# Weight pieces, routing places and scatters in the last attention half chunks: another order on four queues

## The chip, the cores and the metric

The kernel runs on one core of one Trainium2 chip. The metric is the device time of one execution in microseconds. Three timed runs of the kernel before are shown, and one more execution was taken with the hardware profiler.

## The reference

Three layers follow each other. What is computed, cut to the core:

```python
# 1. gated linear attention: B, H, S, D = 4, 8, 768, 48
f = 1 / (1 + exp(-f_logit))
for t in range(S):
    state = f[t][:, None] * state + outer(k[t], v[t])
    y[t] = q[t] @ state
x = y.reshape(3072, 384)
# 2. mixture of 8 experts, one per token, skipped where x @ w_skip <= 0
e = argmax(x @ w_gate);  gate_w = softmax(x @ w_gate)[e]
x = x + gate_w * (relu(x @ w1[e]) @ w2[e])
# 3. dense layer of width 2048
h = x @ w_in;  g = h * tanh(softplus(h));  out = g @ w_out
```

## The kernel before, in words

Every engine executes its own instructions in the order in which the program issues them; nothing is reordered. The order is written out by hand.

The attention runs in `attention` (L235 on) over 24 chunks `n` of 128 tokens; each chunk has two half chunks (two pairs of heads each), numbered `d` from 0 to 47. The loop at L676 covers `d` 0 to 43, and the last four are written out behind it (L776 to L812). For a half chunk TensorE does `stage1(d + 2)` (scores, L373, which ScalarE copies out and GpSimd masks, L386) and `stage2(d)` (L418 with the running state `sbd`, then L426 and L438). ScalarE's `evac(d)` (L470) copies the outputs out, VectorE's `state(d)` (L459 to L465) makes the state that `stage2(d + 2)` reads. In program order `state(d - 1)` stands at the head of half chunk `d`. Each even `d` VectorE also makes `kg` and `kh` (L344 to L352), GpSimd makes a query tile (`qh`, L357), and TensorE turns the chunk before into rows (`finalize`, L482 to L490).

Routing goes by groups of chunks (L675): `(first chunk, chunks, half chunk of route1, lag)`. The groups (0, 7), (7, 7) and (14, 4) are ranked at `d` = 17, 31 and 39. There TensorE counts ranks (`rank`), VectorE computes `place` (three small operations, L562 to L564: an expert's limit for each token, and the position of a token without an expert) and `rank_read` (four, L571 to L574, the last one a copy of the position into the token's row). One half chunk later `route2_all` (L590 to L598) gives the slots, and GpSimd's indirect DMAs (`scatter`, issued at L233) write the rows into the DRAM tensor `tokens`, one for each chunk, one per half chunk for a group of seven and two per half chunk for the group of four (`d` = 40 and 41). Chunks 18 to 20 are ranked behind the loop, at `d` = 44, and chunks 21 to 23 later still.

`first_x` (called at `d` = 42) loads the first 128 rows of two experts from `tokens` on SyncE's queue (`load_half`, L853). `transposed` (L840) turns them: three transposes on TensorE, a copy on ScalarE (L848), a residual on VectorE (L849). The attention's call of it stands at `d` = 46. The first expert matmuls (`half1`, L922) read its result.

`Weights` (L70 on) brings weights in chunks of three pieces of 512 columns. `step` makes one piece: ScalarE copies it to a rounded upper part (L131), VectorE subtracts that from the raw piece (L116, 128x512, the residual). A residual is kept pending until the next `step`, so that ScalarE's copy has time; at a chunk's last piece it is not kept, so two residuals stand together there. Steps with `load=False` run at `d` = 34 to 43 (`W_AT`), one at 44, one at 46 and two at 47. `load` issues the next chunks on SyncE's queue as soon as their stage buffer has been read.

Of the kernel before, what the change touches and what calls it, by code (L numbers as in the profile page):

```python
# [15 lines left out]
ALU = mybir.AluOpType  # L16
# [8 lines left out]
NT = B * NC  # L25
# [7 lines left out]
GATE, POS, TOK = DM, DM + 1, DM + 2  # L33
# [31 lines left out]
class Weights:  # L65
# [22 lines left out]
    def load(self):  # L88
        now = self.pieces[self.piece][1] if self.left() else len(self.chunks)
        while self.loaded < min(len(self.chunks), now + len(self.stage)):  # L90
            src, o, width, wide = self.chunks[self.loaded]
            t = self.stage[self.loaded % len(self.stage)]
            s = src[:, o:o + width]
            if wide:
                self.nc.sync.dma_start(out=t.bitcast(U32), in_=s.bitcast(U32))
            else:
                self.nc.sync.dma_start(out=t, in_=s)
            self.loaded += 1
# [19 lines left out]
    def step(self, eng=None, load=True, now=False):  # L118
        nc = self.nc
        eng = eng or nc.vector  # L120
        if not self.left():
            self.flush(eng)
            return
        u, c, o, so, n, last = self.pieces[self.piece]
        wide = self.chunks[c][3]
        st = self.stage[c % len(self.stage)]
        hi_t, lo_t = self.dests[u]
        hi, lo = hi_t[:, o:o + n], lo_t[:, o:o + n]
        if not wide:
            raw = st[:, so:so + n]  # L130
            nc.scalar.copy(hi, raw)  # L131
        self.flush(eng)
        if wide:
            v = st.bitcast(U32)[:, 2 * so:2 * (so + n)].rearrange("p (n t) -> p n t", t=2)
            low, high = v[:, :, 0], v[:, :, 1]
            t = self.tmp["t"]()
            nc.vector.tensor_scalar(t, high, 3, 0x3FFFFFF8, ALU.logical_shift_left, ALU.bitwise_and)
            nc.vector.scalar_tensor_tensor(t, high, 0xC0000000, t, ALU.bitwise_and, ALU.bitwise_or)
            nc.vector.scalar_tensor_tensor(t, low, 29, t, ALU.logical_shift_right, ALU.bitwise_or)
            raw = t.bitcast(F32)  # L140
            if now:
                nc.scalar.copy(hi, raw)
                eng.tensor_tensor(lo, raw, hi.bitcast(F32), ALU.subtract)
        if not (wide and now):
            self.pend = (lo, raw, hi)
            self.late = wide
        self.piece += 1
        if last:
            if not wide:
                self.flush(eng)  # L150
            if load:
                self.load()
# [88 lines left out]
def attention(tc, A, st, weights, open_weights, open_second, first_x):  # L241
    nc = tc.nc
    kqT, fT, v, U = A["kqT"], A["fT"], A["v"], A["U"]
    const = st["const"]
# [8 lines left out]
    pr = tail.enter_context(tc.tile_pool(name="at_pr", bufs=1, space=PSUM, side="right"))  # L253
# [213 lines left out]
    def evac(d):  # L467
        n, h2 = divmod(d, 2)
        ot, _ = ous[d]
        nc.scalar.copy(xts[n % 2][K112, 2 * h2:2 * h2 + 2, :], ot[K112])  # L470
        if h2 == 1:
            del prep[n]
# [83 lines left out]
        row = rows[n // RG][:, n % RG:n % RG + m, :]  # L556
        nc.gpsimd.tensor_copy(row[:, :, TOK:UW].bitcast(U32), tok.to_broadcast([128, m, UW - TOK]))

    def place(n, m):
        oh, pos, oh_lim = rt[n][0], rt[n][3], rt[n][4]  # L560
        p = pos[:, :, 0]
        nc.vector.tensor_tensor(oh_lim, oh, const["lim"][:, 0:m, :], ALU.mult)  # L562
        nc.vector.tensor_tensor(p, oh[:, :, 7], const["rtok"][:, n:n + m], ALU.mult)
        nc.vector.tensor_tensor(p, p, const["place"][:, n:n + m], ALU.add)  # L564

    def rank_read(n, m):
        oh, t, ex, pos, oh_lim = rt[n]
        rk = rks[n]
        t2 = rks[n] = small("t2", m, 8)
        row = rows[n // RG][:, n % RG:n % RG + m, :].bitcast(U32)  # L570
        nc.vector.tensor_tensor(pos[:, :, 0], pos[:, :, 0], rk[:, :, 7], ALU.subtract)  # L571
        nc.vector.tensor_tensor(t, rk, oh_lim, ALU.is_lt)
        nc.vector.tensor_tensor(t2, rk, bc(pos), ALU.subtract)
        nc.vector.tensor_copy(row[:, :, POS], pos[:, :, 0])  # L574

    def route2(n, m):
        oh, t, ex, pos, oh_lim = rt[n]
# [25 lines left out]
    def scatter(n):  # L603
        scatter_rows(tc, "tiles", st, U, st["slot"][:, n:n + 1], rows[n // RG][:, n % RG, :])

    def pad():
        p = pr.tile([1, EARLY], F32, name="pad", tag="fin", bufs=1)
        cum = st["cum"]
        nc.tensor.matmul(p, lhsT=const["ones"][:, 0:1], rhs=cum[:, 0:EARLY], start=True, stop=True)
        nc.vector.tensor_scalar(p, p, -1.0, float(CAP // 2), ALU.mult, ALU.add)  # L610
        c = cum[0:1, 0:EARLY]
        nc.vector.scalar_tensor_tensor(c, p, 0.0, c, ALU.max, ALU.add)
# [63 lines left out]
    for d in range(ND - 4):  # L676
        n, h2 = divmod(d, 2)
        if d - 4 in SIGMOID_AT:
            table(LN_EXP)
        ranked = [r for r in group if d == r[2] + r[3]]  # L680
        fresh = h2 == 0 and 0 < n < NT - 2 and d - 2 not in SIGMOID_AT
        if fresh:
            recip(n + 2)
        while h2 == 0 and asked < min(NT, n + (3 if d < QUERY_AT else 4)) and ready(asked, d):
            qh(asked)
            asked += 1
        if d > 0:
            state(d - 1)
        if fresh:
            kg(n + 2)  # L690
            kh(n + 2)
        if d - 1 in SIGMOID_AT:
            kg(n + 3)
            kh(n + 3)
        if d > 0:
            if d == 2:
                keep_warm(14)
            stage1(d + 2, all(d - i not in SIGMOID_AT for i in (1, 2)))
        for r in group:
            if d == r[2] + 1:  # L700
                route_exp(*r[0:2])
        if h2 == 0 and n >= 1:
            finalize(n - 1)
        stage2(d)
        if d == 0:
            keep_warm(3)
            stage1(2, True)
        for r in ranked:
            rank(*r[0:2], d=d)
        evac(d)  # L710
        for r in ranked:
            place(*r[0:2])
            rank_read(*r[0:2])
        for d0, pair in SIGMOID_AT.items():
            if d0 < d < d0 + 4:
                for i, p in ((0, 0), (0, 2)) if d == d0 + 1 else ((1, 2 * (d - d0 - 2)),):
                    sigmoid(pair[i], p, p + 2)
            for hh, at in zip(pair, SCAN_AT[d0]):
                if d - d0 in at:
                    p = 2 * at.index(d - d0)  # L720
                    scan(hh, p, d % 2)
                    scan(hh, p + 1, d % 2)
                if d - d0 == at[1]:
                    ends(hh)
        if d in SIGMOID_AT:
            recip(n + 3)
            if asked == n + 3:
                qh(asked)
                asked += 1
            table(SIGMOID)  # L730
        if d == 0:
            ends(0)
            qh(2)
            asked = 3
        if d == 1:
            scan(1, 2, 0)
            scan(1, 3, 0)
            kg(2)
            kh(2)
            ends(1)  # L740
            const.update(route_consts(tc, st["cp"], wk))
        if d % 6 == 1 and d // 6 + 2 < NH:
            load(d // 6 + 2)
        if d in F_AT:
            load_f(4 + F_AT.index(d))
        if d in ZERO_AT:
            zero(ZERO_AT.index(d))
        if d == LOAD_AT:
            weights.load()
        if d == CLOSE_AT:  # L750
            early.close()
            open_weights()
        if d == SECOND_AT:
            mid.close()
            open_second()
        if d in W_AT:
            weights.step(load=False)
        if d in LOADS_AT:
            weights.load()
        for r in group:  # L760
            if d == r[2]:
                route1(*r[0:2])
            elif d == r[2] + r[3] + 1:
                route2_all(*r[0:2])
            elif d == r[2] + 1:
                tokens(*r[0:2])
        if d == ND - 5:
            pad()
        if d == ND - 6:
            x = first_x()  # L770
        for r in group:
            for i in range(r[1]):
                if d == r[2] + r[3] + 1 + (i // 2 if r[1] == 4 else i):
                    scatter(r[0] + i)
    st["x0T"] = [wk.tile([128, KD, 128], F32R, name=f"x0T{i}") for i in range(2)]
    d = ND - 4  # L776
    route1(NT - 6, 3)
# [21 lines left out]
    d += 1  # L799
    stage2(d)  # L800
    evac(d)
    transposed(tc, st, pr, x[0][:, 0, :], *st["x0T"], slice(0, 128), "ut")
    finalize(NT - 2)
    weights.step(load=False)
    d += 1
    stage2(d)
    evac(d)
    for i in range(2):
        weights.step(load=False)
# [6 lines left out]
    finalize(NT - 1)  # L816
    route1(NT - 3, 3)
    route_exp(NT - 3, 3)
    place(NT - 3, 3)
    tokens(NT - 3, 3)  # L820
    yield
    rank(NT - 3, 3)
# [805 lines left out]
```

## Time and profile before

| | us |
|---|---|
| median of 3 runs | 724.15 |
| lowest and highest run | 721.01, 724.60 |
| the profiled execution | 722.45 |
| its span, first to last instruction | 720.1 |
| TensorE matmul busy | 686.9 (95%) |
| VectorE, ScalarE, GpSimd busy | 529.5, 500.1, 166.5 |

The page gives times of the profiled execution; the 2.35 us between its span and its time lie outside the instructions. The attention with its tail takes the first 154 us. Times in views are microseconds from the span's start. PE is TensorE, DVE VectorE, ACT ScalarE, POOL GpSimd, SP SyncE. An entry in square brackets is the idle time of the engine before the instruction, with what ended it.

### The profile page before, as it was taken

Reading aid. Unit: us, or ns where it says so; the run is one execution under the profiler, and the core shown is the slowest. Engines: PE = TensorE matmul, PEld = TensorE weight load, DVE = VectorE, ACT = ScalarE, POOL = GpSimd, SP = SyncE. Lnnn points to the kernel's source line nnn. Section 1 sums busy time; section 2 is a strip of 40 time slices with the busy share of each in tenths; the row PEclk is TensorE's granted clock in tenths of the full one; section 3 lists DMA queues with packets and bytes.
Section 4 is the critical chain, followed back from the end, with each engine's and each line's share of the span. In section 5 each row is a group of like instructions: output and inputs, shape, how many; then the busy total and the mean of one; then the engine's idle time right before and its main releaser. Section 6 shows DMA issues by size and latency. Waiting matters only on the chain.

```text
span 720.1 us, 13033 instructions
## 1 busy us (share of the span) xinstructions
PE 686.9 (95%) x5000; PEld 618.7 (86%) x5000; DVE 529.5 (74%) x1049; ACT 500.1 (69%) x857; POOL 166.5 (23%) x219
## 2 busy tenths in 40 slices
PE   6988889799999999999999999999999999999994
PEld 3777777687999999989998999999999999989994
DVE  6678889977668889879988875766556656666571
ACT  5689778566656654398989867767776686658671
POOL 4643857634001111212222220200020001002002
PEclk8999999899999999999999999999999999999998
DMA  9577834358468874602241112212232133100001
GB/s 351 231 285 268 337 127 174 133 166 294 148 232 263 272 281 154 231 25 88 88 132 45 44 45 89 88 49 84 89 132 87 45 94 127 45 1 34 11 1 48
DMA packets 24790, 97.88 MB, mean 136 GB/s; under 512 B 3476, under 2 KB 10080, under 8 KB 23696
## 3 DMA queue, kind: packets, MB, share of 16 engines
q1 hardware_dynamic: 20272, 83.88, 34.0%
q0 software_dynamic: 4448, 13.09, 4.9%
q8 instruction: 41, 0.67, 0.4%
q14 instruction: 29, 0.24, 0.1%
HBM read 81.88 MB, written 15.84 MB: 136 GB/s over the span
## 4 chain that ended last, share of the span: by engine, by line
PE 73%; issue 1%; DVE 1%; DMA 1%; POOLq 0%; POOL 0%; ACT 0%
PE y L1144 28%; PE h L1094 27%; PE y L908 8%; PE h L893 7%; PE pt L847 2%; PE h L922 1%; DMA x<-tokens 1%; PE h L934 0%; POOLq L1624 0%; DVE hs L1107 0%; DVE wB L849 0%; POOL tokens L233 0%; DVE wB L848 0%; POOLq L1571 0%; DVE gl L1127 0%
## 5 line engine op out<-in xcount | busy, mean ns | idle before, releaser
L1108 ACT ACTIVATE sp<-hs 128x512 f32<-128x512 f32 x96 | 59.7, 628 | 73.6 <-DVE hs L1107 72.8
L1094 PE MATMUL h<-wB,wB 128*128 128x512 f32 x432 | 108.9, 396 | 0.0
L1094 PE MATMUL h<-wB,wA 128*128 128x512 f32 x432 | 106.8, 393 | 0.0
L1144 PE MATMUL y<-wD,gh 128*128 128x384 f32 x384 | 98.9, 339 | 0.0
L1144 PE MATMUL y<-wA,gh 128*128 128x384 f32 x384 | 97.6, 335 | 0.0
L1125 DVE TENSOR_TENSOR hs<-hs,sp 128x512 f32<-128x512 f32 x96 | 69.8, 727 | 32.5 <-ACT sp L1119 32.4
L1094 PEld LDWEIGHTS h<-wB,wA 128*128 128x128 f32 x432 | 80.3, 188 | 14.3
L1094 PEld LDWEIGHTS h<-wB,wB 128*128 128x128 f32 x432 | 79.5, 188 | 14.5
L1107 DVE COPY hs<-h 128x512 f32<-128x512 f32 x71 | 48.9, 688 | 41.0 <-PE h L1094 40.8
L1127 DVE TENSOR_TENSOR gl<-hs,gh 128x512 fp32r<-128x512 f32 x96 | 67.3, 701 | 13.5 <-PE y L1144 6.4
L1144 PEld LDWEIGHTS y<-wA,gh 128*128 128x128 f32 x384 | 70.0, 188 | 4.2
L1144 PEld LDWEIGHTS y<-wD,gh 128*128 128x128 f32 x384 | 70.5, 188 | 3.4
L1144 PE MATMUL y<-wD,gl 128*128 128x384 f32 x192 | 65.1, 339 | 0.0
L1144 PE MATMUL y<-wA,gl 128*128 128x384 f32 x192 | 64.5, 336 | 0.0
L1115 ACT ACTIVATE sp<-sp,tiny 128x512 f32<-128x512 f32 x96 | 61.8, 713 | 0.3
L373 PE MATMUL at<-qi,kh 48*128 48x176 f32 (+1 forms) x384 | 43.5, 348 | 10.1 <-DVE lg L490 6.5
L1119 ACT ACTIVATE sp<-sp 128x512 f32<-128x512 f32 x96 | 52.9, 621 | 0.3
L233 POOL DMA_INDIRECT out<-stage,idx x24 | 23.8, 993 | 124.7 <-ACT stage L1163 62.1
L1126 DVE CAST gh<-hs 128x512 fp32r<-128x512 f32 x96 | 48.8, 509 | 3.3
L877 ACT ACTIVATE mhh<-h 128x256 fp32r<-128x256 f32 x64 | 23.7, 383 | 32.9 <-PE h L893 25.8
L373 PEld LDWEIGHTS at<-qi,kh 48*128 48x128 f32 x384 | 31.2, 201 | 15.8 <-POOL qi L357 3.4
L1173 POOL COPY idx<-rows 128x2 uint32<-128x2 uint32 x12 | 3.3, 290 | 156.5 <-DMA rows<-tokens 156.5
(216 smaller groups left out, 1443.7 us busy)
## 6 DMA issues: line engine op xcount, KB each, us to landing
stage<-in_w SPq DMA_DIRECT2D x64, 768.0 KB, 4.5
kq<-in_kqT SPq DMA_DIRECT2D x6, 1536.0 KB, 6.8
rows<-tokens SPq DMA_DIRECT2D x16, 388.0 KB, 5.1
fb<-in_fT SPq DMA_DIRECT2D x8, 768.0 KB, 9.4
vb<-in_v SPq DMA_DIRECT2D x7, 576.0 KB, 9.5
tokens<-zeros SPq DMA_DIRECT2D x4, 776.0 KB, 9.3
kq<-in_kqT SPq DMA_DIRECT2D x2, 1024.0 KB, 9.2
kq<-in_kqT SPq DMA_DIRECT2D x2, 512.0 KB, 7.8
```

Of the source, the lines that this page charges most:

```text
L373: nc.tensor.matmul(at[:, j, a * QW:a * QW + w], lhsT=k[r, p, :], rhs=q[r, p, 0:w], start=True, stop=True)
L893: nc.tensor.matmul(h, lhsT=w[:, o:o + 128], rhs=x[:, k, :], start=(k == 0 and i == 0), stop=(k == KD - 1 and i == 2),)
L908: nc.tensor.matmul(ys[e, a], lhsT=h, rhs=w[:, ws], start=(f == 0 and i == 0), stop=(f == NE - 1 and i == 2),)
L1094: nc.tensor.matmul(h, lhsT=w[:, o:o + 128], rhs=x[:, k, :], start=(k == 0 and i == 0), stop=(k == KD - 1 and i == 2),)
L1107: (nc.scalar.copy if busy(s) else nc.vector.tensor_copy)(hs, h)
L1108: nc.scalar.activation(out=sp, in_=hs, func=AF.Sigmoid, scale=-1.0)
L1115: nc.scalar.activation(out=sp, in_=sp, func=AF.Ln, bias=st["tiny"])
L1119: nc.scalar.activation(out=sp, in_=sp, func=AF.Tanh, scale=-1.0)
L1125: nc.vector.tensor_tensor(hs, hs, sp, ALU.mult)
L1126: nc.vector.tensor_copy(gh, hs)
L1127: nc.vector.tensor_tensor(gl, hs, gh.bitcast(F32), ALU.subtract)
L1144: nc.tensor.matmul(ys[b][a], lhsT=g[:, a * 128:(a + 1) * 128], rhs=w, start=(first and i == 0), stop=(fs[-1] + 1 in ends and i == len(ins) ...
```

## The change

Five edits, all in the order or the engine of small work:

- `rank_read` writes the position into the row by a subtraction of its own, first of the four operations, where a copy stood last.
- `place` runs on GpSimd for the groups ranked at `d` = 17, 31, 39 and 44; the last group keeps VectorE.
- A chunk's last residual is kept pending like the others in steps with `load=False`; `load` flushes it if its stage buffer is about to be overwritten.
- The four scatters of the group (14, 4) go one at `d` = 40, two at 41, one at 42, and `first_x` at 42 stands behind them.
- The first rows are turned at `d` = 47 between `stage2` and `evac`, where they were turned at 46 behind `evac`.

```diff
     def load(self):
         while self.loaded < min(len(self.chunks), now + len(self.stage)):
+            if self.pend is not None and self.pieces[self.piece - 1][1] == self.loaded - len(self.stage):
+                self.flush(self.nc.vector)
...
         if last:
-            if not wide:
+            if not wide and (load or eng is not nc.vector):
                 self.flush(eng)
...
-    def place(n, m):
+    def place(n, m, eng=nc.gpsimd):
-        nc.vector.tensor_tensor(oh_lim, oh, const["lim"][:, 0:m, :], ALU.mult)
-        nc.vector.tensor_tensor(p, oh[:, :, 7], const["rtok"][:, n:n + m], ALU.mult)
-        nc.vector.tensor_tensor(p, p, const["place"][:, n:n + m], ALU.add)
+        eng.tensor_tensor(oh_lim, oh, const["lim"][:, 0:m, :], ALU.mult)
+        eng.tensor_tensor(p, oh[:, :, 7], const["rtok"][:, n:n + m], ALU.mult)
+        eng.tensor_tensor(p, p, const["place"][:, n:n + m], ALU.add)
...
     def rank_read(n, m):
+        nc.vector.tensor_tensor(row[:, :, POS], pos[:, :, 0], rk[:, :, 7], ALU.subtract)
         nc.vector.tensor_tensor(pos[:, :, 0], pos[:, :, 0], rk[:, :, 7], ALU.subtract)
         nc.vector.tensor_tensor(t, rk, oh_lim, ALU.is_lt)
         nc.vector.tensor_tensor(t2, rk, bc(pos), ALU.subtract)
-        nc.vector.tensor_copy(row[:, :, POS], pos[:, :, 0])
...
+        for r in group:
+            for i in range(r[1]):
+                if d == r[2] + r[3] + 1 + ((i + 1) // 2 if r[1] == 4 else i):
+                    scatter(r[0] + i)
         if d == ND - 6:
             x = first_x()
-        for r in group:
-            for i in range(r[1]):
-                if d == r[2] + r[3] + 1 + (i // 2 if r[1] == 4 else i):
-                    scatter(r[0] + i)
...
     evac(d)
-    transposed(tc, st, pr, x[0][:, 0, :], *st["x0T"], slice(0, 128), "ut")
     finalize(NT - 2)
     weights.step(load=False)
     d += 1
     stage2(d)
+    transposed(tc, st, pr, x[0][:, 0, :], *st["x0T"], slice(0, 128), "ut")
     evac(d)
...
-    place(NT - 3, 3)
+    place(NT - 3, 3, nc.vector)
```

## Rows read from the trace of the kernel before

**Rows 1.** Busy time of each engine by stretch; instructions in brackets, granted clock behind
```profile
core 0: us, PE busy (x) PEld busy (x) DVE busy (x) ACT busy (x) POOL busy (x), PEclk, DMA share, GB/s
117.30:132.40 15.10, 13.91 (x226) 11.46 (x221) 13.85 (x31) 13.59 (x28) 14.17 (x15) 1.00 0.35 121
132.40:135.60 3.20, 0.00 (x0) 0.00 (x0) 3.20 (x4) 0.79 (x2) 2.36 (x3) 1.00 0.15 56
135.60:143.40 7.80, 7.18 (x76) 6.55 (x78) 7.45 (x23) 3.78 (x8) 3.63 (x4) 0.56 0.46 154
143.40:153.60 10.20, 10.20 (x177) 8.82 (x173) 8.17 (x36) 6.68 (x16) 5.02 (x7) 1.00 0.47 157
```

**Rows 2.** Waits of PE, 118 to 154 us: total, times, longest
```profile
PE ou L418 <- DVE sbd L465: 3.3, 1, 3.3
```

**Rows 3.** Timeline of DVE, 128 to 136 us: start, duration, what, count
```profile
128.47 1.48 DVE L116 TENSOR_TENSOR wB<-stage,wB 128x512 fp32r<-128x512 f32 x1
129.88 0.34 DVE L465 TENSOR_TENSOR sbd<-ou,sbd 112x192 f32<-112x192 f32 x1
130.14 0.35 DVE L562 TENSOR_TENSOR ohl<-oh,lim 128x32 f32<-128x32 bf16 x1
...
131.71 3.60 DVE L116 TENSOR_TENSOR wB<-stage,wB 128x512 fp32r<-128x512 f32 x2
135.23 0.34 DVE L465 TENSOR_TENSOR sbd<-ou,sbd 112x192 f32<-112x192 f32 x1
```

**Rows 4.** Line 116's instructions: duration in ns, least, median, most
```profile
L116 DVE TENSOR_TENSOR wB<-stage,wB x36: 678/683/2564, 117.1 to 251.2; 128x512 fp32r<-128x512 f32 x36
```

**Rows 5.** Timeline of POOL, 128 to 136 us
```profile
128.09 1.28 POOL L357 TENSOR_TENSOR qi<-kq,fb 112x512 f32<-112x512 f32 x1
129.31 1.13 POOL L386 TENSOR_SCALAR_AFFINE_SELECT am<-am 128x512 f32<-128x512 f32 x1
...
131.83 0.66 POOL L386 TENSOR_SCALAR_AFFINE_SELECT am<-am 128x512 f32<-128x512 f32 x1
132.44 1.27 POOL L357 TENSOR_TENSOR qi<-kq,fb 112x512 f32<-112x512 f32 x1
133.66 1.10 POOL L386 TENSOR_SCALAR_AFFINE_SELECT am<-am 128x512 f32<-128x512 f32 x1
```

**Rows 6.** Groups of POOL to 160 us by shape: busy us, mean ns, idle before
```profile
L357 POOL TENSOR_TENSOR qi<-kq,fb 112x512 f32<-112x512 f32 x24 | 31.2, 1301 | 4.3 <-DVE fb L297 3.6 <-DMA kq<-in_kqT 0.5
...
L318 POOL TENSOR_SCALAR f<-eend 112x4 f32<-112x4 f32 x8 | 1.8, 223 | 0.7
...
L557 POOL CAST xr<-tok 128x8 uint32<-128x8 f32 x1 | 0.2, 213 | 0.0
```

**Rows 7.** Timeline of POOL and DVE around the ranking at half chunk 17
```profile
68.52 0.65 POOL L386 TENSOR_SCALAR_AFFINE_SELECT am<-am 128x512 f32<-128x512 f32 x1 [0.65 <-ACT am L383]
...
69.09 0.21 DVE L562 TENSOR_TENSOR ohl<-oh,lim 128x56 f32<-128x56 bf16 x1
...
69.69 0.16 DVE L571 TENSOR_TENSOR pos<-pos,ou 128x7 f32<-128x7 f32 x1
```

**Rows 8.** Timeline of DVE at the ranking of half chunk 31
```profile
108.81 0.16 DVE L571 TENSOR_TENSOR pos<-pos,ou 128x7 f32<-128x7 f32 x1 [0.17 <-ACT xts L470]
```

**Rows 9.** Timeline of ACT and PE where the first expert matmuls start
```profile
151.49 0.48 ACT L848 CAST x0T<-pt 128x384 fp32r<-128x384 f32 x1
...
153.59 0.38 ACT L470 COPY xts<-ou 112x256 f32<-112x256 f32 x1
...
154.02 0.74 PE L922 MATMUL h<-wB,x0T 128*128 128x512 f32 x2 [0.34 <-ACT xts L470]
```

**Rows 10.** Timeline of POOL and SP: last scatter of group (14, 4), first row loads
```profile
143.47 0.98 POOL L233 DMA_INDIRECT tokens<-xr,slot  x1 [0.30 <-issue]
...
146.54 0.80 SPq L853 DMA_DIRECT2D x<-tokens  x2
```

**Rows 11.** DMA issues of the page: count, KB each, median us to landing
```profile
x<-tokens SPq DMA_DIRECT2D x2, 194.0 KB, 2.5
```

## The prediction

> **What bounds the kernel now.** I read the busy time by stretch first. From 117.3 to 132.4 us POOL is busy 14.17 of 15.10 us, PE 13.91, DVE 13.85 and ACT 13.59: four full queues that feed each other. From 132.4 to 135.6 PE does nothing at all. From 135.6 to 143.4 PE is busy 7.18 of 7.8 us, but for 76 matmuls only, and its granted clock is 0.56, so mostly the lower level of 1.2 GHz, right behind that idle time; DVE is busy 7.45 us there. From 143.4 PE is busy without a gap at the full clock [rows 1]. So the place where a reordering can gain is the gap and what follows it. Secondly the waits of PE: in 118 to 154 us its one long wait is 3.3 us, in the second state matmuls (L418) for `sbd` of L465 [rows 2].
>
> The timeline of DVE then shows what stood ahead of that L465: the `state` of half chunk 38 ends at 130.22, `place` and `rank_read` of 39 run from 130.14 to 131.71, and then two residuals take 3.60 us instead of two times 0.68, the first of them 2.56 [rows 3, 4]. The timeline of POOL says why: the masking L386 and the query product L357 run back to back from 131.83 to 133.71, and DVE's first residual ends 0.56 us behind them, at 134.27; the second ends behind the next L386, which itself took 1.10 instead of 0.66 [rows 3, 5]. The residual of 128.47 tells the same: it ends at 129.95, 0.58 behind POOL's L357 (129.37), and POOL's next L386 is stretched to 1.13 [rows 3, 5]. So an operation of DVE on two SBUF tiles and POOL's work exclude each other, and the loser waits for whole instructions.
>
> **Part by part.** *Place on POOL, half chunk 39.* DVE loses three small operations, 0.6 us by those of half chunk 17 (69.09 to 69.69, [rows 7]). POOL gets three, of a kind without a row of its own. From below: 3 x 0.21, the small cast and scalar operations there [rows 6], 0.63 us. From above: these plus the slope of L357, (1.30 - 0.21) / 512 = 2.1 ns for each of up to 56 elements, 0.33 a piece, 1.0 us. I take 0.8, nearer to the small rows, since two of the three have 7 elements or fewer. POOL is in order, so they stand behind the masking of the same half chunk, which ends at 132.49 [rows 5]: places are ready at 133.3. `rank_read` on DVE waits for them, and queued behind it are the residual and the `state` of half chunk 39, for which PE waits. DVE, which worked from 130.22 on, now idles until 133.3. Then `rank_read` (four of at most 0.16 [rows 7], taken as 0.5) to 133.8, and one residual instead of two. By then POOL runs the query product, moved by the 0.8 from 132.44 to 133.3, to 134.55; the residual ends 0.56 behind it, at 135.1. The state, 135.23 before, starts at 135.05: **-0.2 us**. What the second residual would have cost (1.04 of the 3.60) is given up to the wait for places. Ends: if the residual loses to the next mask too, as it did to two in a row at 131.71, that adds 0.65, so +0.5. If POOL comes to 39 earlier by a stretched instruction or two (0.45 each, 1.10 or 1.13 against 0.66), state starts 0.9 earlier, and the gap may be short enough for the clock to stay: -0.9 minus the price of the clock.
>
> That price: the matmuls of 135.6 to 143.4 took 7.18 us at 0.56 and would take 4.0 at full clock, but DVE was busy 7.45 of the 7.8 us, so between 0.35 and 3.2 us [rows 1]; I take 1.5, near the middle, because no row favours an end.
>
> The Trainium skill ("SBUF — State Buffer", section "Who interferes with whom") says that whoever issues first gets the shared port pair for its whole instruction, and the other blocks. The residual issued at 131.71, ahead of the mask at 131.83, lost to it and to L357 behind it [rows 3, 5], so the trace doesn't bear the rule out there; by the rule the residual would end at 135.1, by the row at 135.75. The skill's "GPSIMD Engine Reference" (section "Engine selection") speaks against the edit: elementwise work with two inputs is about 2x slower on GpSimd. By that, an estimate from the 0.6 us of DVE, places take 1.2 us, and the sum would be 0.8 higher (0.4 at 17 and at 39); no row shows such an operation on POOL.
>
> *Place on POOL, half chunks 17, 31, 44.* At 17 POOL's mask ends at 69.17, so places are ready at 69.97, and `rank_read` starts at 70.05 instead of 69.69 [rows 7]: **+0.36**, ends 0.2 and 0.55 by the two prices; all on DVE's path, and I find no idle time of DVE soon behind it that would take it up; below nothing is excluded, as DVE would only wait. At 31 POOL is free long before; but DVE's L571 waits for ACT's L470 there in any case, 0.17 us [rows 8], so the time freed turns into a longer wait: 0, at best the -0.6 of the operations if that wait belongs to another cause. At 44 PE is busy throughout [rows 1]: 0; if DVE's relief shows or POOL's place is late, within 0.3 either way.
>
> *No two residuals together.* The count of residuals is unchanged; those of pieces 2, 5 and 8 move one step later. At 36 one moves away and at 37 one is added before `route1`, where POOL is just as full; it delays DVE by about one residual, 0.7 us, up to half chunk 38, where the residual waits for POOL's L357 in any case [rows 3, 5]: 0. If that cover is gone, 0.7 us. At 40 residual 5 now stands before `route2_all`, so slots and the next states come 0.7 us later; PE, slow there, hides it, and at full clock some 0.4 would show. SP's loads of the next chunks wait one step longer; their pieces are used several steps later: 0.
>
> *Positions without a copy.* Four operations before, four after, each 0.16: 0. The first instead of the last writes the row and reads PSUM, so it can't collide with POOL: between -0.3 and 0.
>
> *Scatters one, two, one.* Each takes POOL 0.98 us [rows 10]. One moves from 40 to 41 and one from 41 to 42. Masks for the following half chunks come earlier by one scatter at 41 and are otherwise unmoved. The last scatter starts some 1.2 us later, by the 0.7 of the slots and about 0.5 of POOL's order: 144.7 instead of 143.47. SP's `first_x` started 3.07 us behind the last scatter (146.54) [rows 10] and lands 2.5 us after issue [rows 11]: 147.8 and 150.3. What is queued behind it on SP are chunk loads, not urgent.
>
> *First rows turned later.* PE does the same transposes one `finalize` and one `stage2` later, about 1.7 us, at 152.6: 2.3 us behind the landing. ACT's copy (0.48) now stands before `evac` of 47 instead of well ahead of it; PE's first expert matmul waited for that `evac` (153.59 + 0.38, then 154.02) [rows 9]. In the old order ACT was itself held up by DVE's residual of the first rows, which now comes later, so I expect the row copy from about 0.5 us earlier, the new copy to 153.65 and `evac` to 154.0: **+0.1**, ends 0 and +0.5 (the whole copy on the path).
>
> **Sum:** -0.2 + 0.36 + 0 + 0.1 = +0.25 us. The profiled execution's 722.45 would be 722.7; the median of the runs lies 1.7 above that execution, so 724.15 becomes **724.4**.
>
> **Rivals.** *The gap closes.* If POOL's places came before DVE needs them at 39 (POOL ahead by about 2.5 us, or places issued while POOL waits for something), one residual without a collision would put the state at about 132.5. The gap of 3.3 us and the price of the clock, 1.5, go: -4.8, so 719.35. For it: two residuals of 3.60 us are the direct cause of the gap. Against it: POOL has no free time from 117.3 on [rows 1], and the mask ahead of the places ends at 132.49 [rows 5].
>
> *Half of it.* POOL comes 0.9 us earlier and the clock stays up: -0.9 - 1.5 and the rest of the sum, +0.45: 722.2, still within 0.5%.
>
> *Slower: the first rows come too late.* The last scatter, `first_x` behind it and the transposes are now one chain, and `evac` of 47 stands behind the transposes' copy on ACT. If the landing comes after 152.6, PE waits, and nothing else is queued on it. It decides from 2.3 us of delay on: one more POOL collision for each of the three scatters and two masks ahead (5 x 0.45) and a scatter slower to land by 2.3 would make it 2.3 us late, and a second fall of the clock costs up to another 1.5: 724.4 + 3.8 = 728.2. Against it: the margin, and POOL's idle time in this stretch (5.02 of 10.20 busy, [rows 1]).
>
> **How the numbers follow.** Forecast 0.55 (with the ends of its costs, 722.7 to 726), the gap closes 0.2, half of it 0.12, too late 0.13. A measurement of this kernel tells about 0.5%, 3.6 us, from no change. The gap closing is the one case beyond it on the fast side, the late rows on the slow side: faster 0.2, same 0.67, slower 0.13. The range takes in the gap closing with the -0.6 of half chunk 31, 718.8, and most of the way to the late rows, 727.2.
>
> **What would show it.** Right: PE still waits over 2 us for L465 near 133 to 135.5, DVE's idle time before the first `rank_read` operation is ended by POOL, the residual behind it still takes over 1 us, and the clock falls behind it. At 17, DVE waits about 0.4 us for POOL. Wrong: places on POOL of 0.1 us or of 0.5 us each; a residual of 0.68 at 39 and no gap; PE waiting for x at the late transposes; or a fall of the clock at another place.

## The result and the profile after

| | before | after |
|---|---|---|
| median of six runs each, us | 724.07 | 731.18 |
| lowest and highest, us | 720.97 to 724.60 | 726.94 to 733.63 |
| ratio, 95% interval | | 1.0104 [1.0066, 1.0143] |
| the profiled execution, us | 722.45 | 728.95 |
| its span, us | 720.1 | 727.3 |

The changed kernel is slower by 7.1 us, outside the range of the prediction (718.8 to 727.2). Lines of the changed file stand 2 below those of before (L116 is L118, L465 is L467, L847 is L849).

First the stretch that the prediction was about. Busy time by stretch in the kernel after (columns as in [rows 1]), then the timelines of DVE and of POOL at half chunk 39, which answer to [rows 3] and [rows 5]:

```profile
132.40:135.60 3.20, 2.77 (x42) 2.45 (x38) 2.08 (x7) 1.80 (x5) 3.12 (x6) 0.83 0.17 62
135.60:143.40 7.80, 6.28 (x105) 5.44 (x105) 7.59 (x24) 5.17 (x11) 3.94 (x5) 1.00 0.46 152
```

```profile
133.49 0.16 DVE L573 TENSOR_TENSOR xr<-pos,ou 128x4 uint32<-128x4 f32 x1 [2.31 <-POOL pos L566]
...
133.98 1.24 DVE L118 TENSOR_TENSOR wB<-stage,wB 128x512 fp32r<-128x512 f32 x1
135.15 0.34 DVE L467 TENSOR_TENSOR sbd<-ou,sbd 112x192 f32<-112x192 f32 x1
```

```profile
132.16 0.65 POOL L388 TENSOR_SCALAR_AFFINE_SELECT am<-am 128x512 f32<-128x512 f32 x1
132.78 0.24 POOL L564 TENSOR_TENSOR ohl<-oh,lim 128x32 f32<-128x32 bf16 x1
132.98 0.19 POOL L565 TENSOR_TENSOR pos<-oh,rtok 128x4 f32<-128x4 bf16 x1
133.25 0.20 POOL L566 TENSOR_TENSOR pos<-pos,place 128x4 f32<-128x4 f32 x1
133.40 1.27 POOL L359 TENSOR_TENSOR qi<-kq,fb 112x512 f32<-112x512 f32 x1
```

DVE idles 2.31 us for the places, the one residual behind them still loses to POOL's query product (1.24 us, and its end at 135.22 is 0.55 behind POOL's 134.67), and the state starts at 135.15, where it was 135.23. That is DVE's wait as it was predicted. PE's is another one in this profile: it waits only 0.43 us for that state, because it comes there late itself, with its clock at the lower level from 130.05 to 133.46 us. Nothing is lost up to here: the first expert matmul starts at 154.11 against 154.02 in [rows 9].

The loss lies behind. The waits of PE from 160 to 310 us, before and after (total, times, longest):

```profile
PE pt L847 <- DMA x<-tokens: 1.4, 2, 1.0
```

```profile
PE pt L849 <- DMA x<-tokens: 4.1, 1, 4.1
PE pt L849 <- DMA rows<-tokens: 1.6, 1, 1.6
...
```

Two places, then. *Place 1* is near 174 us: PE waits for `x`, the second halves of the rows of the first two experts, which GpSimd loads behind the last scatters (chunks 21 to 23). The chain that leads there, in the kernel after (start, duration):

```profile
167.92 4.84 issue
172.76 4.90 DMA x<-tokens
...
177.71 0.83 PE pt L849 x3
```

The load of the rows waits from the end of the last scatter's issue (167.92) to its landing, and PE waits for the load, which takes 4.90 us from issue to landing. PE's first transposes come 4.95 us behind its issue; before, they came 2.78 us behind it (174.42 - 171.64). The granted clock is 0.84 from 173 to 184 us (the lower level, 1.2 GHz, from 177.8 on for 3.4 us), where before had 1.00. Before, and below it after:

```profile
173.00:184.00 11.00, 9.56 (x50) 7.96 (x51) 5.01 (x10) 4.85 (x11) 3.51 (x4) 1.00 0.78 284
```

```profile
173.00:184.00 11.00, 6.75 (x28) 5.97 (x28) 4.44 (x9) 3.10 (x7) 4.42 (x6) 0.84 0.78 253
```

*Place 2* is near 300 us: PE waits for `rows`, the first rows of the dense layer (part 3 of the reference). They need the last expert finished by DVE (L943, from 294.57 us), its rows scattered (from 296.66, 4.33 us to the landing) and loaded again (from 301.05, 3.06 us).

The shift between the two profiles can be read at the same work of PE in both (times of before): +0.1 us at the first expert matmul, +3.3 at the first transposes of `x` (174.42 to 177.71), +4.3 at the first transposes of expert rows (187.2 to 191.5, behind the low clock), +4.7 at 278.4, +6.5 at 297.7, +7.2 at 300.0 and at the end of the span. So place 1 costs 4.2 us; of the other 2.9, 0.4 come before 278.4 and 2.5 at place 2.

### The profile page after: what moved, and what is told of

Read it like the earlier page. It is cut to its first block, busy times and chain, and to the rows that moved or that the text cites. A ratio compares the mean times of both kernels' runs of the same rounds, so it can differ in the third digit from the quotient of the medians.

```text
span 727.3 us, 13029 instructions
## 1 busy us (share of the span) xinstructions
PE 688.6 (95%) x5000; PEld 619.5 (85%) x5000; DVE 527.5 (73%) x1038; ACT 499.2 (69%) x857; POOL 169.4 (23%) x230
## 4 chain that ended last, share of the span: by engine, by line
PE 68%; DVE 4%; DMA 2%; issue 1%; ACT 1%; POOLq 0%; POOL 0%; SPq 0%
PE y L1146 28%; PE h L1096 27%; PE y L910 6%; PE h L895 5%; PE pt L849 2%; PE h L924 1%; DVE wt L140 1%; DMA x<-tokens 1%; DVE wt L141 1%; DMA tokens<-rows 1%; DVE wA L118 1%; DVE mhl L883 0%; ACT wA L117 0%; DMA rows<-tokens 0%; DVE wC L118 0%
```

## The experiments

Each kernel was timed against the kernel before on the same chip. The median of before was 723.85 us beside the first four, 723.81 beside the next four and 725.14 beside the last four, so the ratios are what is compared. The start of the expert matmuls differs between profiled executions (152.1 to 157.9 us, with low clock windows at different places of the attention), so marks behind it are given relative to it.

**Where the rows lose.** Both loads of place 1 in the kernel before, POOL's and SP's:

```profile
163.48 0.99 POOL L233 DMA_INDIRECT tokens<-xr,slot  x1 [7.15 <-DVE mhl L881]
164.78 1.05 POOL L233 DMA_INDIRECT tokens<-xr,slot  x1 [0.30 <-ACT wD L131]
166.14 0.98 POOL L233 DMA_INDIRECT tokens<-xr,slot  x1 [0.30 <-issue]
171.64 1.16 POOL L853 DMA_DIRECT2D x<-tokens  x2 [4.52 <-issue]
...
172.58 0.33 SPq L97 DMA_DIRECT2D stage<-in_w  x1
```

And after:

```profile
163.85 0.99 POOL L235 DMA_INDIRECT tokens<-xr,slot  x1 [7.22 <-DVE mhl L883]
165.14 1.49 POOL L235 DMA_INDIRECT tokens<-xr,slot  x1 [0.30 <-issue]
166.94 0.98 POOL L235 DMA_INDIRECT tokens<-xr,slot  x1 [0.30 <-issue]
172.76 1.16 POOL L855 DMA_DIRECT2D x<-tokens  x2 [4.84 <-issue]
...
172.76 0.33 SPq L99 DMA_DIRECT2D stage<-in_w  x1
```

Before, the rows are issued 0.94 us ahead of a chunk of weights (768 KB); after, in the same instant, because the rows come 1.0 us later relative to the first expert matmul and the chunk only 0.1 later. The packets by queue (packets, MB, share of the 16 engines) from 172 to 174 us before, and from 173 to 176 us after:

```profile
q0 software_dynamic: 80, 0.28, 52.9%
q1 hardware_dynamic: 19, 0.04, 4.8%
```

```profile
q1 hardware_dynamic: 100, 0.61, 72.9%
```

Before, GpSimd's queue (software) moves first; after, for three microseconds only SP's queue (hardware) moves, though GpSimd's rows were issued with it. From 176 to 178.5 us the software queue then has 190 packets, beside 44 of SP's. Three experiments move the two loads against each other.

**e1 and e2: the chunk behind the rows**, in the kernel after (e1) and in the kernel before (e2).

```diff
-                self.nc.sync.dma_start(out=t, in_=s)
+                (self.nc.gpsimd if self.loaded in (10,) else self.nc.sync).dma_start(out=t, in_=s)
```

> The changed kernel with one edit: the load of weight chunk 10 is issued on GpSimd's queue, behind the loads of the expert rows, where SyncE issued it at 172.76 us, in the same moment as the first of them. Theory of the race (the weight chunk goes ahead of the rows on the DMA engines): the rows land about 2.5 us after issue instead of 4.9, PE's wait for x falls from 4.1 to about 2 us, and the time falls by 2 to 4 us, to 727 to 729. Rival (the chain of scatters is simply late, and landing is as slow as it is): PE's wait stays near 4 us and the time within 1 us of 731. Rival (late weights cost more than late rows): slower by some us.

e1 measured 728.30 us, 1.0064 [1.0036, 1.0093]. PE's wait for `x` is 1.9 us, its first transposes come 2.85 us behind the issue of the rows, and a wait for `rows` of 1.1 stays. So the order of the two loads is worth some 3 of the 7 us. The rest is not the order: the rows are still issued 0.9 us later than before relative to the first expert matmul, the clock still falls to its lower level for 3.4 us (from 176.5), and place 2 stays.

> The kernel before with the same edit: chunk 10 on GpSimd's queue behind the row loads. Theory of the race: before, the rows had been issued 0.9 us ahead of the chunk, so nothing or up to 1.5 us is gained (722 to 724). If runs of before differ among themselves by this race, the spread of 721 to 724.6 shrinks. Rival of late weights: slower by 1 us or more.

e2 measured 723.10 us, 0.9978 [0.9957, 0.9999], with a wait for `x` of 1.2: where the rows already went first, holding the chunk back gives 0.2%, at the edge of what can be told.

**e3: the kernel before, with the rows issued later**, three tiny loads ahead of them on GpSimd's queue.

```diff
+    scratch = work.tile([1, 24], F32, name="scratch")
+    for i in range(3):
+        nc.gpsimd.dma_start(out=scratch[0:1, i * 8:(i + 1) * 8], in_=U[NTOK + i:NTOK + i + 1, 0:8])
     for e in range(EARLY):
         load_half(tc, A, xin[e], NTOK + e * CAP + 128, 1, nc.gpsimd)
```

> The kernel before with three tiny loads (8 numbers each) issued on GpSimd's queue ahead of the row loads, which delays these by about 1.2 us and changes nothing ahead of them. Theory of the race: SyncE's chunk 10 is now ahead of the rows on the DMA engines, PE's wait for x grows by over 3 us, from 1.4 to about 4.5, and the time by 3 to 5 us, to 727 to 729. Rival (no race, a plain shift): the wait grows by 1.2 us and the time by about 1.2 us, to 725.

Measured: 730.08 us, 1.0078 [1.0050, 1.0106]; PE waits 4.1 us for `x`, as in the kernel after, and not for `rows`. A delay of 1.8 us at this one load, with nothing of the change, makes 5.6 us, more than the 3 to 5 expected. The delay itself is 1.8 of them; the transposes come 1.3 us later behind the issue than before (4.11 instead of 2.78), and the clock falls for 6.8 us from 1.4 us before the end of the wait. With e1 and the packets, this shows place 1 as a race between two queues.

**e4: the kernel after, with places back on DVE everywhere.**

```diff
-    def place(n, m, eng=nc.gpsimd):
+    def place(n, m, eng=nc.vector):
```

> The changed kernel with the places back on VectorE for all groups. If GpSimd's places are what costs, the time goes back to 724. Theory of the race: it depends on where the scatters of the last group and the chunk's load end up, which the places of the groups before don't set: within 2 us of 731. In the attention DVE no longer waits 2.3 us for POOL at half chunk 39, and PE's first state matmul there stays near 135.5 us, as DVE collides with POOL instead.

Measured: 731.33 us, 1.0101 [1.0070, 1.0133], waits of 4.1 for `x` and 1.8 for `rows`: as after. Places by GpSimd have no part in the loss that can be told here.

**e5: the kernel after, with the copy of the position back.**

```diff
-        nc.vector.tensor_tensor(row[:, :, POS], pos[:, :, 0], rk[:, :, 7], ALU.subtract)
         nc.vector.tensor_tensor(pos[:, :, 0], pos[:, :, 0], rk[:, :, 7], ALU.subtract)
         nc.vector.tensor_tensor(t, rk, oh_lim, ALU.is_lt)
         nc.vector.tensor_tensor(t2, rk, bc(pos), ALU.subtract)
+        nc.vector.tensor_copy(row[:, :, POS], pos[:, :, 0])
```

> After, with the position copied into its row by a fourth operation again (as before). Theory A, the missing copy delays the last group's first scatter (9.46 to 9.74 us behind the start of the expert matmuls) and with it the second scatter into a residual of DVE: the second halves of the expert rows are issued 0.3 to 0.7 us earlier, again ahead of the chunk of weights that SP loads near 172.7, the wait of PE for x (4.1) goes back below 2, and the time is 727 to 729. Rival, the order one, two, one of the scatters delays them by itself: issue as in after, the wait stays at 4, the time stays at 731. In both the wait for rows near 300 us stays (1 to 2 us).

Measured: 725.94 us, 1.0038 [1.0014, 1.0062], somewhat better than expected. Its row loads are 0.97 us ahead of the chunk again, and the wait for `x` is as two short ones, while that for `rows` stays:

```profile
PE pt L849 <- DMA x<-tokens: 2.0, 2, 1.0
PE pt L849 <- DMA rows<-tokens: 1.2, 1, 1.2
```

So one copy of 0.16 us, put back, is worth 4.8 us. The reason is seen on DVE before the first of the three scatters. Before, and below it after (the last line of each is the group of three residuals behind):

```profile
161.74 0.13 DVE L571 TENSOR_TENSOR pos<-pos,rk 128x3 f32<-128x3 f32 x1
...
161.91 0.18 DVE L573 TENSOR_TENSOR t<-rk,pos 128x24 f32<-128x24 f32 x1
162.00 0.16 DVE L574 CAST xr<-pos 128x3 uint32<-128x3 f32 x1
162.12 0.18 DVE L580 TENSOR_TENSOR t<-t,rt 128x24 f32<-128x24 f32 x1
162.34 0.18 DVE L581 TENSOR_REDUCE sl<-t 128x3 f32<-128x24 f32 x1
162.55 0.16 DVE L582 TENSOR_TENSOR slot<-sl,pos 128x3 uint32<-128x3 f32 x1
...
163.70 1.89 DVE L116 TENSOR_TENSOR wD<-stage,wD 128x512 fp32r<-128x512 f32 x3
```

```profile
161.92 0.13 DVE L573 TENSOR_TENSOR xr<-pos,rk 128x3 uint32<-128x3 f32 x1
162.09 0.16 DVE L574 TENSOR_TENSOR pos<-pos,rk 128x3 f32<-128x3 f32 x1
...
162.28 0.18 DVE L576 TENSOR_TENSOR t<-rk,pos 128x24 f32<-128x24 f32 x1
162.50 0.18 DVE L582 TENSOR_TENSOR t<-t,rt 128x24 f32<-128x24 f32 x1
...
162.92 0.16 DVE L584 TENSOR_TENSOR slot<-sl,pos 128x3 uint32<-128x3 f32 x1
...
163.86 1.92 DVE L118 TENSOR_TENSOR wD<-stage,wD 128x512 fp32r<-128x512 f32 x3
```

L580 needs the result of L573 and starts 0.21 us behind it, with the copy between the two; L581 and L582 need the one before them too and start 0.22 and 0.21 behind it with nothing between. So the copy stood in a gap and cost nothing. After, the operation that writes the row stands at the head, and the one that updates `pos`, on which the others hang, starts 0.17 us later: from the first operation to the slots 1.00 us instead of 0.81.

These 0.19 us, of 0.28 by which the first scatter is late (9.74 us behind the first expert matmul instead of 9.46), put the second scatter against a residual of DVE. The third of the three residuals L118 runs from 165.10 to 165.78 there (its start lies inside the group that the timeline joins); the scatter comes at 165.14 and takes 1.49 us. Before, the scatter (164.78) is 0.12 ahead of the residual (164.90) and takes 1.05. That adds 0.43 from the first to the last scatter. The last 0.3 us are from the last scatter to the load that waits for its landing, 5.50 before and 5.82 after: the scatter lands 4.9 us behind its start before and 5.2 after, each time 0.6 us ahead of the load. This interval lay between 5.49 and 6.51 us in the profiles (e3, with loads in between, left out), and what sets it was not found. It alone can use up a margin of 0.94 us.

**e6: the kernel after, with the flush ahead of a load left out for wide chunks.** The flush computes the pending residual at once, before the load is issued. The weights of the dense layer come as wide chunks of two pieces, which DVE first puts together in a temporary tile (L139 to L141). Their pending residual reads this tile and not the stage buffer, so that a load needn't wait for it.

```diff
-            if self.pend is not None and self.pieces[self.piece - 1][1] == self.loaded - len(self.stage):
+            if self.pend is not None and not self.late and self.pieces[self.piece - 1][1] == self.loaded - len(self.stage):
```

> After, with the new flush ahead of a load left out where the pending residual belongs to a wide chunk (second product), whose residual reads a temporary tile and not the stage buffer. Theory: DVE no longer waits 0.58 us for ACT's copy (L117) at the last piece of each wide chunk, the last expert of the first group is finished earlier, and PE's wait for rows near 300 us (1.6) goes; the wait for x near 174 to 178 stays at 4.1. Time 728.5 to 729.5, 2 to 2.5 less than after. Rival, DVE is late there only because the whole was shifted against the loads by the first wait: the rows wait stays and the time stays at 731.

Measured: 728.05 us, 1.0065 [1.0042, 1.0088]. The wait for `x` is 4.1, the wait for `rows` gone. DVE's waits from 255 to 310 us for ACT's copy of a wide piece, after and in e6:

```profile
DVE wA L118 <- ACT wA L117: 4.2, 9, 0.6
```

```profile
DVE wA L118 <- ACT wA L117: 1.0, 4, 0.2
```

Before has 1.0 in 4 times as well. How it looks in the timeline of DVE after, right ahead of the finish of the last expert (L943):

```profile
292.54 0.56 DVE L141 SCALAR_TENSOR_TENSOR wt<-stage,wt 128x384 uint32<-128x384 uint32 x1
293.68 0.56 DVE L118 TENSOR_TENSOR wA<-wt,wA 128x384 fp32r<-128x384 f32 x1 [0.58 <-ACT wA L117]
...
294.49 1.14 DVE L943 SCALAR_TENSOR_TENSOR rows<-y,rows 128x384 f32<-128x384 f32 x2
```

The raw piece is finished by L141, ACT only then copies it, and DVE stands idle until the copy is there. In the kernel before it went on and took the residual one piece later.

**e7: the kernel after, with both edits** (e5 and e6).

> After, with both edits: the copy back and the flush left out for wide chunks. If the two places carry the whole difference: PE's wait for x below 2 us, none for rows near 300 us, time 724 to 726, the same as before within 0.3%. If the copy isn't the cause of the first place: 728.5 to 729.5. If something third costs time (places on GpSimd, the order of the first rows), it stays above 726 with neither wait.

Measured: 723.16 us, 0.9979 [0.9955, 1.0004]; wait for `x` 1.1 us, none for `rows`. Places by GpSimd, the residuals one by one in the narrow chunks, the scatters' order and the late turning are all still in it. The two causes carry the whole difference, as far as these runs can tell.

**e8: the kernel before, with the part on residuals alone** (the two edits in `Weights`).

> Before, with the part on residuals alone (no two together, and the flush ahead of a load). Theory: the flush at the last piece of each wide chunk makes DVE wait for ACT's copy and brings the wait for rows near 300 us, which before doesn't have: +1.5 to +2.5 us, 725.5 to 726.5, with the wait for x near 174 us as in before (1.4). Rival, the rows wait comes only with the shift of the first place: no such wait, 724. If the residuals moved past the positions also delay the last group's scatters, the x wait grows to 4 and the time to 730.

Measured: 725.51 us, 1.0031 [1.0004, 1.0058]. Waits of PE from 160 to 310 us:

```profile
PE pt L849 <- DMA rows<-tokens: 1.6, 1, 1.6
PE pt L849 <- DMA x<-tokens: 1.5, 2, 1.0
```

The wait for `rows` comes without the shift of place 1, by the flush alone: +2.2 us. The rival, that place 2 only follows from place 1, is out.

**e9: the kernel after, with the row's position written last instead of first.** Four operations and no copy, as in the kernel after; the updated `pos` goes to a tile of its own.

```diff
-        nc.vector.tensor_tensor(row[:, :, POS], pos[:, :, 0], rk[:, :, 7], ALU.subtract)
-        nc.vector.tensor_tensor(pos[:, :, 0], pos[:, :, 0], rk[:, :, 7], ALU.subtract)
+        pn = small("pn", m, 1)
+        rt[n] = (oh, t, ex, pn, oh_lim)
+        nc.vector.tensor_tensor(pn[:, :, 0], pos[:, :, 0], rk[:, :, 7], ALU.subtract)
         nc.vector.tensor_tensor(t, rk, oh_lim, ALU.is_lt)
-        nc.vector.tensor_tensor(t2, rk, bc(pos), ALU.subtract)
+        nc.vector.tensor_tensor(t2, rk, bc(pn), ALU.subtract)
+        nc.vector.tensor_tensor(row[:, :, POS], pos[:, :, 0], rk[:, :, 7], ALU.subtract)
```

> After, with the same four operations of rank_read and no copy, but the one that writes the position into its row stands last instead of first, and the difference that the others read goes to a tile of its own. If the cost is the place of that operation on the chain of dependent ones: from the first of the four to the slots (L584 to L586) 0.81 us again instead of 1.00, the second scatter 1.04 instead of 1.49, PE's wait for x at most 2, time 725.5 to 726.5, as with the copy back (725.94). If it is the kind of the operation (it reads PSUM) or the missing copy as such: chain 1.00, wait 4.1, time 731.

Measured: 727.26 us, 1.0024 [0.9997, 1.0051] (1.0024 of 724.07 is 725.8). The chain of DVE is 0.81 us again, with the row's operation in the gap:

```profile
164.04 0.13 DVE L575 TENSOR_TENSOR pn<-pos,rk 128x3 f32<-128x3 f32 x1
...
164.30 0.15 DVE L578 TENSOR_TENSOR xr<-pos,rk 128x3 uint32<-128x3 f32 x1
...
164.85 0.16 DVE L586 TENSOR_TENSOR slot<-sl,pn 128x3 uint32<-128x3 f32 x1
```

The second scatter takes 1.07 us, and PE's first transposes come 2.88 behind the issue of the rows. So it is the place in the chain, not the missing copy or the operand in PSUM. One expectation failed: PE's wait for `x` was 3.1 us in two waits, not at most 2. The second of the two row loads still came late (a wait of 1.8), with the first one only 0.76 us ahead of the chunk. The profiled execution was one of the longer ones (728.83 of 723.12 to 729.28).

**e10: the kernel before, with the positions without a copy alone.**

> Before, with the positions without a copy alone. If this part is enough for the first place: chain 1.00 us, x rows issued 0.1 to 0.3 us beside or behind the weight chunk, PE's wait for x 3 to 4.1 instead of 1.4, time 727 to 728.5 (half chunk timing else as in before), no wait for rows near 300 us. If it takes the other parts too (fewer residuals ahead of the scatters): wait below 2, time 724.

Measured: 729.21 us, 1.0055 [1.0026, 1.0085], which is +4.0 us by the ratio. So this part alone is enough for place 1. The second scatter meets the residual here too, and PE waits 4.4 us for `x` (3 to 4.1 expected), none for `rows`:

```profile
167.58 0.99 POOL L233 DMA_INDIRECT tokens<-xr,slot  x1 [7.18 <-DVE mhl L881]
168.87 1.49 POOL L233 DMA_INDIRECT tokens<-xr,slot  x1 [0.31 <-issue]
170.67 0.98 POOL L233 DMA_INDIRECT tokens<-xr,slot  x1 [0.30 <-issue]
177.18 1.17 POOL L853 DMA_DIRECT2D x<-tokens  x2 [5.53 <-issue]
```

In this profile the rows are 1.6 us later than before, relative to the first expert matmul. 0.6 of it are the chain and the collision; the other 1.0 is the interval from the last scatter to the load, 6.51 us here.

**e11: the kernel before, with the places by GpSimd alone.**

> Before, with the places by GpSimd alone. By the prediction's own terms: DVE waits for POOL at half chunks 17 (0.4 to 0.7 us) and 39, where two residuals still stand behind rank_read and lose 3 us to POOL, so that L465 comes 1 to 1.5 us later than in before; time 724.5 to 726. If places free DVE in a stretch where it is the bound: 721 to 723.5. If it delays the last group's scatters too: x wait of 4 and 729 or more.

Measured: 725.93 us, 1.0009 [0.9982, 1.0037], no change that can be told. In its profile PE waits 4.0 us for L465 at half chunk 39 instead of 3.3: with two residuals still behind `rank_read`, the wait for places adds to them. The rows are issued 6.01 us behind the last scatter there, only 0.45 ahead of the chunk, and PE waits 2.5 us for `x`, though the scatters come no later than before.

**e12: both edits of e7, and the chunk behind the rows as in e1.**

> After, with the copy back, the flush left out for wide chunks, and chunk 10 loaded on GpSimd's queue behind the two loads of rows. Each of the three has taken a wait away without adding one, so the x wait is 1.0 to 1.3 us and the rows wait 0; time 721.5 to 723.5, ratio to before 0.995 to 0.999. If the order of these loads decides only where rows would lose the race (they no longer do): 723.2, as without it.

Measured: 725.42 us, 1.0003 [0.9978, 1.0028], above the 721.5 to 723.5 expected: nothing gained over e7, so the order of these loads only counts where the rows would lose. No version here beats the kernel before by more than 0.5%.

**All profiles together.** How far ahead of the chunk the rows were issued, and how long after their issue PE's first transposes of them started (both from the timelines of POOL, SP and PE):

| kernel | rows ahead of chunk, us | issue to transposes, us |
|---|---|---|
| e5, e7, before, e8 | 0.97, 0.98, 0.94, 0.90 | 2.79, 2.87, 2.78, 2.72 |
| e9 | 0.76 | 2.88 |
| e11 | 0.45 | 3.79 |
| e6, e4, after | 0.15, 0.09, 0.00 | 5.06, 4.98, 4.95 |
| e10, e3 | -0.71, -0.83 | 4.46, 4.11 |
| e1, e2, e12 | the chunk is queued behind the rows | 2.85, 2.88, 2.88 |

Rows that lead by 0.15 us or less come 4.9 to 5.2 us behind the issue of the chunk (4.95 - 0.00, 5.06 - 0.15, 4.46 + 0.71), whenever they were issued. With a lead of 0.45 (e11) they come 3.3 us behind it, in between. By ratio, the part on positions alone is +4.0 us, the part on residuals alone +2.2, the places alone +0.7 (with an interval that holds zero); together 6.9 of the 7.5 that 1.0104 is. Each of the three is known to some 2 us either way.

## Why the prediction was wrong

**What held, up to 154 us.** *Half chunk 39*: places predicted at 132.49 to 133.3 after the mask, found at 132.78 to 133.45 behind a mask that ended at 132.81; price 0.8 taken, 0.63 found, at the lower end. The residual behind it was to end 0.56 behind POOL's product, and did at 0.55. State at 135.05 forecast, 135.15 found, so -0.1 in place of -0.2. *Half chunk 17*: DVE waits 0.73 us for POOL there (0.4 forecast), whose three operations take 0.29, 0.21 and 0.21. The scan behind `rank_read` starts 1.62 us behind L465, where it started 1.26 behind L463 before: +0.36, as forecast. *Half chunk 31*: the wait for ACT's L472 grew to 0.64 us ([rows 8] had 0.17), as said. *Scatters*: the last of the group at 144.76 (144.7 forecast), `first_x` at 147.78 (147.8). *Late turning*: at 152.72 without a wait (152.6), the copy to 153.79 (153.65), `evac` of 47 to 154.06 (154.0), the first expert matmul 0.09 later (0.1). The rival "the gap closes" had no ground: POOL came to half chunk 39 no earlier. One sign was not met in the profile after: PE's wait for the state of half chunk 39 was 0.43 us and not over 2. In e1, e5, e6, e7, e9 and e12, with the same order there, it was 2.0 to 2.3.

**A term that was off without effect: the clock.** The prediction let it fall behind half chunk 39 and priced it at 1.5 us, between 0.35 and 3.2. In the profile after, the lower level lay ahead of that, from 130.05 to 133.46, and the matmuls of 135.6 to 143.4 ran at 1.00; in e5, e6, e9 and e12 it lay behind the state of half chunk 39 for 6.8 us, as forecast. From the start of that state to the first expert matmul it is 18.96 us after and 19.01 to 19.03 in those four. So the price was under 0.1 us, below its lower end (154.11 - 135.15 after; 153.89 - 134.86 in e5). DVE is busy 7.59 of the 7.80 us after and PE 6.28, so DVE is the busier there and PE's clock matters little.

**A reading that left a line out.** The prediction read the residual issued at 131.71, ahead of the mask at 131.83, as one that started first and lost. [rows 5] leave out that POOL's scatter (L233) ran from 130.78 to 131.81. An operation of POOL was under way when the residual started, so these rows don't settle who goes first.

**The steps that failed.** *"Positions without a copy. Four operations before, four after, each 0.16: 0."* The count was right and the cost was not: the operations aren't worth their durations but their places in a chain of dependent ones. The removed copy had filled a gap of 0.21 us; the added operation stands ahead of the chain, +0.19. With the lower end given as -0.3 and the upper as 0, even the sign was excluded. The row for it, the operations near 162 us, was in the trace of before, where the copy stands in the gap.

The second failure is that *the sum ended at the first expert matmul*. `rank_read` runs once more, at about 162 us, for the last group, and its scatters, the row loads behind them and SP's chunk make a chain beside the expert matmuls that the prediction never read: 0.19 us became 0.28 at the first scatter, 0.7 with the collision of the second, 1.0 at the row loads, 3.2 at PE and 4.2 with the clock. The margin of that race, 0.94 us, could be read in the profile before.

The third is *"No two residuals together. The count of residuals is unchanged"*: it costed the edit in `step` for the narrow chunks and passed over the one in `load`, whose condition holds at the end of each wide chunk too, up to 300 us. What the runs showed there are nine waits of up to 0.58 us on DVE, 4.2 us where there were 1.0, and 2.2 us (e8) to 2.8 (after less e6) of time.

**The rival that had the right side.** "The first rows come too late" (728.2, 0.13) named late rows and a second fall of the clock, and both came; but it named the first halves on SP's queue, which had a margin and kept it, and as cause POOL's collisions in the attention. The rows that were late are the second halves on GpSimd's queue. So its price, 3.8 us, is near the 4.2 of place 1 without having explained it, and place 2 was in no case at all. That is why 0.67 stood on no change and the range ended at 727.2.

The Trainium skill ("GPSIMD Engine Reference", section "Engine selection") would have had the places at 1.2 us as an estimate; POOL's three took 0.63 us at half chunk 39 and 0.71 at 17, against DVE's 0.54 at 17 (0.21, 0.16 and 0.17), so for tiles of 4 to 56 elements the trace doesn't bear the factor of two out.

## What to carry to other kernels

Follow an edit of a shared helper to each of its uses, the late and covered ones too: the loss lay at the last of five uses of `rank_read` and at a guard that fires in another kind of chunk, both outside the stretch that the change was aimed at. Weigh a small operation by its place between dependent ones and not by its duration: one in a gap is free, one at the head of the chain is paid in full. And where two queues issue loads within a microsecond of each other, read the margin from the timeline and put the urgent load ahead by the program, as on one queue, because 0.2 us on an engine far up the chain can otherwise turn into 4.

## What the hardware did that was not expected

**Two loads issued together are not shared out evenly.** With the rows 0.00 to 0.15 us ahead on GpSimd's queue and the chunk on SP's, the rows came behind most of the chunk; in the kernel after, all 100 packets from 173 to 176 us were of the hardware queue. With a lead of 0.76 us and more the first load of rows went first. The Trainium skill ("DMA: Bandwidth & Descriptors", section "Queues, rings and completion order") says that a DMA engine takes turns between the queues, but by whole packets, several descriptors long, so that it drains one before it switches. The traces here fit that if a packet of the view is one such descriptor, as 100 of one queue in a row are six or seven for each of the 16 engines; they show also that GpSimd's load needed a lead to go first: 0.15 us was too little, 0.45 (e11) gave transposes 3.79 us behind the issue, and 0.76 gave 2.88.

**A scatter's issue on POOL is held up by a residual on DVE that started just ahead of it.** The second scatter took 1.49 to 1.50 us in after, e1, e4, e6 and e10, each time 0.04 us behind the start of a residual, and 1.04 to 1.07 in the nine other profiles, where it came 0.10 to 0.13 ahead of one. The Trainium skill ("SBUF — State Buffer", section "Who interferes with whom") has it that the one that starts first keeps the shared ports for its whole instruction and the other blocks. The trace bears that out in one direction only: the scatter that came second lost 0.45 us, but before, the residual that came 0.12 us behind the scatter kept its 0.68.

**The lower clock came with PE's wait for `x`, but not only with the longest.** The granted clock fell to its lower level there in seven profiles: in after, e3, e4, e6 and e10, where PE had stood still for 4.1 to 4.4 us, but also in e1 (1.9) and e11 (2.5). It began between 1.4 us before and 0.5 us behind the end of the wait and lasted 3.4 us, in e3 6.8. From the first transposes of `x` to the first of expert rows it was 13.6 to 13.9 us with a fall of 3.4, and 12.5 in e2, e7 and e12 with neither a fall nor a second wait, so the fall cost 1.1 to 1.4 us. Why it fell in e1 and not in e9 (two waits, 1.3 and 1.8) stays open.
